# Moving filler matmuls, two input loads and a row of weight loads in a fused spectral-mixer and MLP training step

## The chip, the cores and the metric

The kernel runs on one core of a Trainium2 chip. The metric is the device time of one execution in microseconds (us), taken as the median of several runs. Before the change three runs gave 359.58, 359.83 and 359.80 us, a median of 359.8 us.

## The reference

The reference computes one block of a network and all its gradients. `S` is 2048 and `D` is 448, everything is in bf16.

```
def _A_ref(x, w_r, w_i):                      # spectral mixer
    X = rfft2(x); X = X * (w_r + 1j * w_i); return irfft2(X)
def _B_ref(x, w1, b1, w2, b2):                # MLP over the token axis
    h = layernorm(x)
    u = gelu(einsum("bsd,sf->bdf", h, w1) + b1)
    return transpose(einsum("bdf,fs->bds", u, w2) + b2)
h  = x + _A_ref(layernorm(x), A_w_r, A_w_i)
h2 = h + _B_ref(layernorm(h), B_w1, B_b1, B_w2, B_b2)
# outputs: h2 and the gradients of x, w_r, w_i, w1, b1, w2, b2 for a given grad_out
```

## The kernel before

**Tiling.** A Fourier transform of length 2048 over the tokens is done in two steps with small matrices. The first step works on 16 "rows" `t` (128 tokens each): `row_a(t)` multiplies the folded row with a 128x128 matrix, `row_b(h)` multiplies the result with the cosine and sine tables `csF`. The results are copied out of PSUM and sent by a DMA from one layout in SBUF to another, into `D2` (line 668, eight DMAs; the fifth to eighth read from `rX`). The second step is `s2_stage` (line 671). It works on four sets `s`; for each set, `four` issues 48 small matmuls of 32x32 on `D2` into four PSUM tiles, these are copied out as `x`, VectorE multiplies them with the spectral weights into `y` (`w_mult`, eight operations for each set), and a second `four` does the inverse step of the set on `y`. The result is copied out and sent by DMA into `D3` (line 697, four DMAs for each set). `inv_rows` then reads `D3`, and every row of it needs all four sets.

The backward pass runs the same stages once more on the gradient, with `bwd_mult` in place of `fwd_mult`: eight further VectorE operations for each set give the gradient of the spectral weights.

**Order of the work.** TensorE, VectorE, ScalarE and the DMA queue of SyncE (SP) run in the order in which the program is written. Nearly all DMAs stand in SP's one queue, the transposing loads too, and an instruction that waits there holds all that is behind it. Which of VectorE and ScalarE copies a PSUM tile out is decided by a planner (`Meter`, `evac`), from estimated loads. Reshuffle DMAs are put into SP's queue a little later than their data is asked for (`defer`, 1.1 us of the program's own clock, which advances with each matmul that is written).

**Fillers.** `fill(n)` issues the next `n` steps of work that is independent of the stage at hand. In the forward pass that is `dg_gen` (line 791): 14 blocks of 16 matmuls of 128x448, 224 steps in all. Block `j` reads the transposed weight tile `w2T` number `j`, and when it is finished its buffer is loaded with a later tile (five buffers; past the eighth load, the loads are held back until line 907 and are then put into the queue). After the four sets, `fill(24)` and `drain()` issue whatever is left. In the backward pass the fillers are `gw_gen` (line 1228): 15 units of 28 steps with matmuls of up to 512 columns, 420 steps, whose results are copied out and stored to DRAM. `drain()` after the last inverse row issues what is left of these.

**Numbers that place the fillers.** `s2_stage(get_x, on_mult, n1, n2, gap)` issues, for each `s` from 0 to 4: the `four` of set `s`, `fill(n1)`, the inverse `four` of set `s-1`, the weight product of set `s`, `fill(n2)`; and `fill(gap)` at the end. So `n1` fillers stand ahead of each inverse `four`, and `n2` behind it.

Before the change the forward steps are used so: 87 up to and with the `fill(6)` of line 905, 5 x (8 + 10) = 90 in the sets, and 47 in `fill(24)` and `drain()`. In the backward pass: 24 in the last rows, 30 before the sets, 5 x (14 + 22) + 24 = 204 in the sets and after them, 16 x 8 = 128 in `inv_rows`, and 34 in the last `drain()`.

**Loads at the start.** `load_x(q)` (line 313) loads a quarter of x (four rows, 448 KB) and `load_w2T` (line 306) loads and transposes a 512 KB tile. VectorE takes the statistics of rows 6 and 7 at step `t = 0` of the row loop, those of rows 8 and 9, the first of `load_x(2)`, at `t = 1` (`STATS`, line 858). `W_AT` (line 860) says how many of the 18 loads of the spectral weights (line 573) are put into the queue at each step of the row loop.

## Time and profile before

| | us |
|---|---|
| median of three runs | 359.8 |
| time of the profiled execution | 358.56 |
| its span, first to last instruction | 356.8 |
| TensorE matmul busy (x2810) | 331.0 (93%) |
| VectorE busy | 251.1 (70%) |
| ScalarE busy | 196.6 (55%) |
| DMA moved | 78.03 MB, mean 219 GB/s |
| mean granted TensorE clock | 0.981 |

Times within the profile are counted from the first instruction, so they end at 356.8; the execution's own time is 1.76 us longer than the span. In the profile's lines PE is TensorE, DVE is VectorE, ACT is ScalarE, SPq is SyncE's DMA queue. Tiles stand under the names of their SBUF regions: `r<-rX` is a reshuffle into `D2`, `r<-r` at line 697 one into `D3`; `ps_mm<-rC,rE` and `ps_mm<-rC,rO` are the forward fillers, which read `w2T` from `rE` or `rO`; `rX` is also the region of `x`, and `rS` that of `y`. Helpers record their callers' work under one line: 218 for ordinary matmuls, 223 for the 32x32 ones of `four`, 82 for ScalarE and VectorE.

### The profile page before, as it was taken

To read this page: it belongs to the slowest core of one execution; us is meant where nothing else is said; L and a number is where in the kernel's file an instruction comes from. 1 tells how busy PE (TensorE), PEld (TensorE's weight loads), DVE (VectorE), ACT (ScalarE), POOL (GpSimd) and SP (SyncE) were. 2 spreads that over 40 slices of the span, in tenths; PEclk is the share of its full clock that TensorE was granted. 3 is DMA by queue.
4 is the path that set the end of the run, shared out by engine and by line. 5 is a ranking of instruction groups with operands and counts; after the bars stand their busy time and mean duration, and the time that the engine had idled before them with its cause. 6 is when DMAs were issued, how large, how long until landed. Compare 5 with 4: busy or idle time off the path is not lost.

```text
span 356.8 us, 7788 instructions
## 1 busy us (share of the span) xinstructions
PE 331.0 (93%) x2810; PEld 173.6 (49%) x2819; DVE 251.1 (70%) x666; ACT 196.6 (55%) x431; POOL 63.6 (18%) x219
## 2 busy tenths in 40 slices
PE   8569929989999999999999999999999999999992
PEld 3336615445654555555555555564334344466541
DVE  8897426871594788858323888877497986489993
ACT  5448533543796653532331245557468786488972
POOL 5767000000122000001000211110000000046761
PEclk9989978999999999999999999999999999999998
DMA  8998898856995999779785789774988998999864
GB/s 206 287 198 193 165 252 183 173 109 197 317 260 218 296 347 253 173 193 287 170 206 148 169 186 181 169 128 144 248 233 211 267 262 253 238 296 271 268 241 155
DMA packets 147247, 78.03 MB, mean 219 GB/s; under 512 B 95688, under 2 KB 139976, under 8 KB 147080
## 3 DMA queue, kind: packets, MB, share of 16 engines
q1 hardware_dynamic: 146920, 77.13, 84.6%
q8 instruction: 22, 0.36, 0.4%
q10 hardware_dynamic: 288, 0.39, 0.3%
q14 instruction: 17, 0.14, 0.1%
HBM read 25.71 MB, written 22.04 MB: 134 GB/s over the span
## 4 chain that ended last, share of the span: by engine, by line
PE 77%; DVE 7%; SPq 5%; ACT 4%; issue 2%; DMA 2%; DVEq 0%; POOL 0%; ACTq 0%
PE ps_mm L218 65%; PE ps_ff L218 8%; DVE r L82 4%; PE ps_ff L223 3%; SPq L306 3%; ACT rO L82 2%; DVE rS L82 2%; DMA rA<-in_A_x_dram 1%; SPq L573 1%; DVE rA L82 1%; DMA r<-rX 1%; ACT rX L82 1%; SPq L316 1%; SPq L668 1%; ACT rAT L82 0%
## 5 line engine op out<-in xcount | busy, mean ns | idle before, releaser
L218 PEld LDWEIGHTS <-r 128*128 128x128 bf16 (+2 forms) x600 | 56.0, 105 | 44.9 <-issue 2.3
L218 PEld LDWEIGHTS <-rS 128*128 128x128 bf16 (+2 forms) x496 | 40.2, 98 | 39.7 <-issue 6.3
L218 PE MATMUL ps_mm<-rD,r 128*128 128x448 bf16 x224 | 44.5, 352 | 0.0
L82 ACT CAST rO<-ps_mm 128x512 bf16<-128x512 f32 (+1 forms) x66 | 35.5, 583 | 14.4 <-PE ps_mm L218 11.8
L218 PEld LDWEIGHTS <-rst 128*128 128x128 bf16 (+1 forms) x320 | 23.5, 97 | 30.7 <-issue 13.6
L218 PE MATMUL ps_mm<-rC,rE 128*128 128x448 bf16 x144 | 33.4, 369 | 2.0 <-DMA rC<-in_grad_out_dram 1.9
L218 PE MATMUL ps_mm<-rB,r 128*128 128x448 bf16 x160 | 31.2, 352 | 0.1
L218 PE MATMUL ps_mm<-rG,rst 128*128 128x512 bf16 (+1 forms) x122 | 26.7, 380 | 0.5 <-issue 0.3
L82 ACT CAST r<-ps_ff 128x452 bf16<-128x452 f32 x41 | 22.6, 587 | 8.2 <-PE ps_ff L223 5.9
L218 PE MATMUL ps_mm<-r,rst 128*128 128x512 bf16 (+2 forms) x144 | 27.1, 345 | 0.0
L82 DVE SCALAR_TENSOR_TENSOR r<-ps_mm,b2col,r 128x448 bf16<-128x448 f32 x16 | 10.9, 682 | 19.9 <-PE ps_mm L218 16.9
L82 ACT ACTIVATE r<-ps_mm,rstd_h 128x448 bf16<-128x448 f32 x16 | 10.2, 634 | 26.8 <-PE ps_mm L218 26.8
L82 ACT ACTIVATE r<-rC 128x448 bf16<-128x448 bf16 x16 | 9.1, 571 | 26.7 <-DMA out_dram<-r 21.1
L82 ACT ACTIVATE rG<-rG 128x896 bf16<-128x896 bf16 x14 | 13.3, 950 | 14.9 <-DVE rG L82 14.7
L218 PE MATMUL ps_mm<-rE,rS 128*128 128x448 bf16 x112 | 21.5, 352 | 0.0
L218 PEld LDWEIGHTS <-rO 128*128 128x128 bf16 (+1 forms) x165 | 15.2, 98 | 12.3 <-ACT rO L82 0.2
L82 ACT CAST rS<-ps_ff 128x512 bf16<-128x512 f32 x31 | 17.9, 581 | 5.3 <-PE ps_ff L218 5.0
L218 PEld LDWEIGHTS <-rE 128*128 128x128 bf16 x144 | 13.9, 102 | 13.1 <-issue 4.3
L82 ACT CAST rG<-ps_mm 128x512 bf16<-128x512 f32 (+1 forms) x33 | 16.5, 544 | 6.6 <-PE ps_mm L218 6.4
L1135 POOL TENSOR_SCALAR lcol<-lcol 128x1 f32<-128x1 f32 x16 | 8.5, 529 | 64.7 <-ACT r L82 64.7
L218 PE MATMUL ps_ff<-csI,rAT 113*128 113x224 bf16 (+1 forms) x108 | 19.0, 298 | 0.6 <-ACT rAT L82 0.4
L1308 POOL TENSOR_SCALAR lcol<-lcol 128x1 f32<-128x1 f32 x16 | 5.3, 332 | 75.9 <-ACT r L82 75.8
(189 smaller groups left out, 606.0 us busy)
## 6 DMA issues: line engine op xcount, KB each, us to landing
out_dram<-rO SPq DMA_DIRECT2D x34, 256.0 KB
r<-in_B_w_dram SPq DMA_DIRECT2D x5, 1024.0 KB
r<-r SPq DMA_DIRECT2D x32, 113.0 KB
rS<-in_B_w_dram SPq DMA_DIRECT2D x4, 896.0 KB
r<-r SPq DMA_DIRECT2D x12, 226.0 KB
out_dram<-rG SPq DMA_DIRECT2D x10, 256.0 KB
rO<-in_B_w_dram SPq DMA_DIRECT2D x2, 1024.0 KB
rC<-in_grad_out_dram SPq DMA_DIRECT2D x4, 448.0 KB
```

The source lines that it names most:

```text
L82: fn(**kw)
L218: nc.tensor.matmul(out, lhsT=lhsT, rhs=rhs, start=start, stop=stop)
L223: nc.tensor.matmul(out, lhsT=lhsT, rhs=rhs, start=start, stop=stop)
L306: nc.sync.dma_start_transpose(out=wT, in_=B_w2[j * P:(j + 1) * P, :].rearrange("f (t c) -> f t c", c=P))
L316: nc.sync.dma_start(out=go_tp[:, 4 * q:4 * q + 4, :], in_=go_tp_d[:, 4 * q:4 * q + 4, :])
L573: nc.sync.dma_start(out=d_ap if store else sb, in_=sb if store else d_ap)
L668: defer(RESH_LAG, lambda: resh[0].dma_start(out=D2[u:u + 125:4, 8 * e:8 * e + 8].rearrange("p g c k -> p (g c k)"), in_=cs.rearrange("p x ...
L1135: gp_.tensor_scalar(out=m1, in0=ms, scalar1=-1.0 / D, scalar2=None, op0=ALU.mult)
L1308: gp_.tensor_scalar(out=m1, in0=ms, scalar1=-2.0 / D, scalar2=None, op0=ALU.mult)
```

## The change

1. The third and fourth quarters of x are asked for ahead of the second and third `w2T` tiles; before, each came behind one of them.
2. The loads of the spectral weights start at step 0 of the row loop in place of step 1, so that each stands one step earlier; there are 18 as before.
3. Thirty fillers are issued between the rows and the first forward set, and `n1` of the forward sets is 9 in place of 8. The sum of steps is fixed: 117 now stand before the sets, 5 x (9 + 10) = 95 in them, and 12 are left for `fill(24)` and `drain()`, 35 fewer than before.
4. In the backward sets `n1` is 13 in place of 14 and `n2` is 20 in place of 22. That is 15 steps fewer in the sets; the last `drain()` has 49 in place of 34.

```diff
     load_go(2)
     load_go(3)
+    load_x(2)
+    load_x(3)
     load_w2T()
-    load_x(2)
     load_w2T()
-    load_x(3)
     gtail = rst[0:16, 2 * P:3 * P]
...
-    W_AT = {t: 2 if t % 2 else 1 for t in range(1, 13)}
+    W_AT = {t: 1 if t % 2 else 2 for t in range(12)}
...
     while held_w2:
         held_w2.pop(0)()
+    fill(30)
...
-    s2_stage(lambda s: set_of(Xs, s), fwd_mult, 8, 10, 0)
+    s2_stage(lambda s: set_of(Xs, s), fwd_mult, 9, 10, 0)
     sc.activation(out=warm, in_=eps_h, func=ACT.Sqrt)
     fill(24)
     drain()
...
-    s2_stage(lambda s: X_ring.next(), bwd_mult, 14, 22, N_FILL_B[4], ...
+    s2_stage(lambda s: X_ring.next(), bwd_mult, 13, 20, N_FILL_B[4], ...
```

More of the change, by code (lines that the diff above doesn't have):

```diff
@@ L1287 @@
     Meter.slack = 7.0
-    s2_stage(lambda s: X_ring.next(), bwd_mult, 14, 22, N_FILL_B[4], {0: lambda: load_du(1), 1: lambda: (load_du(0), load_xall(0)), 2: lambda: load_xall(1), 3: lambda: load_du(2)},
+    s2_stage(lambda s: X_ring.next(), bwd_mult, 13, 20, N_FILL_B[4], {0: lambda: load_du(1), 1: lambda: (load_du(0), load_xall(0)), 2: lambda: load_xall(1), 3: lambda: load_du(2)},
              2.0 * INV_SD)
```

## The prediction

> **What bounds the kernel now.** I read the page's busy slices first (8.92 us each), then TensorE's waits, then SP's queue and TensorE's timeline around the longest wait, last the sums over stretches.

> ```profile
> PE   8569929989999999999999999999999999999992
> PEclk9989978999999999999999999999999999999998
> ```

> TensorE is full from slice 7 on. It is idle in the first three slices and above all in slice 6 (44.6 to 53.5 us). The granted clock is low there and just behind. TensorE's waits name the cause:

> ```profile
> PE ps_ff L223 <- DMA r<-rX: 6.9, 1, 6.9
> PE ps_ff L218 <- DVE rX L82: 3.0, 1, 3.0
> ```

> The first is the start of the forward sets, which wait for `D2`; the second is row 5 of the row loop. SP's queue shows why `D2` is late (start, length, line):

> ```profile
> 44.96 1.91 SPq L573 DMA_DIRECT2D rW<-in_A_w_i_dram  x3
> 46.97 0.58 SPq L668 DMA_DIRECT2D r<-r  x1
> 47.60 1.91 SPq L573 DMA_DIRECT2D rW<-in_A_w_i_dram  x3
> 49.61 2.57 SPq L668 DMA_DIRECT2D r<-rX  x4
> 52.28 4.24 SPq L306 DMA_TRANSPOSE rO<-in_B_w_dram  x2
> 57.56 5.71 SPq L306 DMA_TRANSPOSE rE<-in_B_w_dram  x2
> 63.37 2.89 SPq L697 DMA_DIRECT2D r<-r  x4
> ```

> SP issues without a gap from 0.73 us on, so the reshuffles that TensorE finished computing at 44.5 go out at 49.6 to 52.2. At the other end of the sets:

> ```profile
> 78.86 0.38 PE L223 MATMUL ps_ff<-rS,UVT 32*32 32x452 bf16 x16 [1.14 <-DVE rS L82]
> 79.50 7.93 PE L218 MATMUL ps_mm<-rC,rE 128*128 128x448 bf16 x41
> 87.27 3.19 PE L218 MATMUL ps_mm<-rC,rO 128*128 128x448 bf16 x16
> 90.29 0.83 PE L218 MATMUL ps_ff<-RTm,r 128*113 128x128 bf16 x12
> ```

> The last inverse group ends at 79.5, then 57 fillers (10 of `n2`, 47 left over) run for 10.8 us, 0.19 us each, and only then `inv_rows` starts, though the last `D3` reshuffle had landed at 88.4 (the trace's DMA semaphores). So fillers are short at 46.6 and in surplus at 79.5. From 107 on TensorE is busy in nearly every microsecond, so a start of `inv_rows` that is earlier moves everything behind it. The stretches below (PE busy first) show the clock, then the backward pass:

> ```profile
> 19.18:22.59 3.41, 1.01 (x10) 0.74 (x11) 3.19 (x12) 0.89 (x1) 2.60 (x11) 1.00 0.82 199
> 22.59:26.00 3.41, 3.40 (x16) 1.71 (x14) 3.34 (x14) 2.12 (x4) 1.35 (x8) 0.50 1.02 197
> 53.31:56.72 3.41, 3.23 (x54) 1.78 (x55) 2.14 (x4) 0.97 (x2) 0.00 (x0) 0.50 0.99 225
> 278.70:288.70 10.00, 9.79 (x148) 4.03 (x149) 8.88 (x19) 7.79 (x16) 0.00 (x0) 1.00 0.90 265
> 307.50:341.30 33.80, 33.80 (x259) 19.62 (x258) 29.95 (x90) 27.62 (x72) 18.02 (x51) 1.00 0.99 278
> ```

> A stretch in which TensorE was busy 30% (19.18 to 22.59) is followed by one at half clock; the stretch before it, busy 1.91 of 3.42 us, 56%, was not. The half clock at 53.31 costs the first set some 1.5 us.

> **x ahead of w2T.** In the trace DMAs land in the order of issue: the last `load_go` 13.99, w2T 1 at 16.8, x 2 at 18.2, w2T 2 at 20.2, x 3 at 22.0. A quarter of x takes 1.2 to 1.4 us when it follows a plain load, a w2T 2.1 to 2.9. After the change: x 2 at 15.3, x 3 at 16.5, w2T 1 at 19.1, w2T 2 at 21.3. VectorE, idle from 16.83 to 18.24 for x 2, goes on 1.4 us earlier. But TensorE meets its second filler block at 17.07, and that needs w2T 1: it now waits 2.0 us, and `row_b(0)`, two fillers and `row_a(5)` are queued behind. `row_a(5)` was at 21.58 and has its operand at 20.1. The half-clock stretch should move from 22.59 to 19.18. Together TensorE is 0 to 1.4 us ahead in the rows. None of it is on the path, because SP sets when `D2` lands. [...]

> **Weight loads a step earlier.** 18 issues of 0.61 us. They precede the fifth `D2` reshuffle in both orders, so SP has the same work ahead of the seventh, which set 0 needs (issued 50.98, landed 53.36). Nothing gained; the sets start at 53.5. Bounds: 0.7 us earlier (w2T 2 lands at 21.3 where x 3 landed at 22.0) and 0.4 later (the small loads go out at 19.2, not 18.85).

> **Thirty fillers before the sets.** 30 x 0.19 = 5.7 us, from 46.6 or up to 1.4 earlier, so to 50.9 to 52.3. They read w2T 5 to 7, loaded by 47. Of the 6.9 us wait 1.2 to 2.6 us stay. The filler time itself is taken from the surplus behind the sets, so its worth is counted there. The clock: 49.9 to 53.3 would then be busy 30 to 70%, between the row that dropped (30%) and the one that didn't (56%), mostly nearer to the second; I take full clock, and 1.5 us for the other end. [...]

> The fillers also call for w2T 10 to 13 sooner: SP now has six transposing loads in a row at 52.3, where two stood between `D3` reshuffles. Four of them took 1.87 to 2.18 us each: 52.3 + 6 x 2.0 = 64.3 for the reshuffles of set 0 (63.4 before), + 2.9, + 3.4 for the bias transposes, + 2.9, + 2.9 = 76.4 behind set 2. Set 3 asks at 78, so SP is free by then; before it was not (its reshuffles of sets 2 and 3 went out in one run from 79.19 to 84.75).

> **The sets.** VectorE sets their pace: from one `y` to the next are the rest of an inverse group, 0.68 us, two copies 1.16, products 3.9, together 5.67 (67.47, 73.14, 78.81). TensorE's 18 fillers and two groups are about 5.1, so a ninth filler at `n1` goes into its waits (0.39, 0.32, 1.14). Only in set 0 does TensorE set the pace: at full clock 53.5 + 0.7 + 19 x 0.19 + 0.7 + 9 x 0.19 = 60.2 for the first inverse group, in place of 61.5; y of set 3 then at 77.3, last group ended at 78.0. At half clock it is 79.75.

> **The drain.** 22 fillers, 4.2 us, end at 82.2. `D3` of set 3: first copy done 78.6, four issues of 0.71 to 81.45, landing 2.7 to 3.6 us after the last (88.39 - 84.75 with the w1 loads right behind, as they will be): 84.2 to 85.1. I take 85.1, the row in the same place. So TensorE waits some 2.9 us for `D3` and `inv_rows` starts at 85.15 in place of 90.29: **-5.1 us** (-5.9 with the early landing; -3.4 at half clock). If that wait empties a clock stretch, `inv_rows` pays up to 1.5 us.

> **Backward sets.** TensorE is busy 9.79 of 10.0 us in a set; VectorE's own loop (6.93 from copies to `y`, 1.93 for the rest of the weight gradient) is 8.9. Three fillers of 0.216 us fewer make TensorE's set 9.35, still the longer. So the sets end 15 x 0.216 = 3.2 us earlier, and `drain()` after the last row is 3.2 us longer: TensorE's sum is unchanged, and it was the last to end (350.5, with VectorE's row chain at 350.65, which now ends sooner). At the junction the last `D3` landed at 306.7 for a start at 307.5; two fillers (0.4 us) fewer cover it, and SP is issuing without a gap there. I take **+0.3 us**, bounds -0.3 (end of VectorE's chain) and +1.0. The planner may hand copies to the other engine; one misplaced in VectorE's forward loop is 0.6 us, taken at nothing.

> **Sum.** 358.56 - 5.1 + 0.3 = 353.8 for a profiled execution; the median of the runs stood 1.24 above it: **355.0 us**.

> **Rivals.** (a) Both waits that remain cost clock: the first set stays at half clock (-3.4) and `inv_rows` starts with 1.5 us lost: 359.8 - 3.4 + 1.5 + 0.3 = 358.2. For it: the row at 30%; against it: both waits are shorter than that one. (b) The backward sets turn out to wait for VectorE: they do not shorten, and the 3.2 us come on top of the end: 358.2. Against it: 0.45 us of slack for each set by the sum above, 1.4 us at the last one (y at 296.31, group at 297.67). (c) Slower: SP. Six transposing loads, 16 reshuffles of 0.71, biases 3.4 and landing 3.6 make `inv_rows` start at 52.3 + 6T + 18.5; this passes 90.29 at T = 3.25 us. At T = 3.7, the longest in the row stage, it starts at 93.0: 362.5 us. For it: 3.37, 3.51, 3.68 and even 6.88 were seen beside other traffic; against it: 2.0 for the four in this very place.

> **How the numbers follow.** Forecast 0.66, (a) 0.16, (b) 0.09, (c) 0.09. Low end: early landing, `D2` 0.7 sooner: 359.8 - 6.6 + 0.3 = 353.5. The high end takes in (a) and (b) at 358.2; (c) stays outside. Differences below 0.2% (0.7 us) can't be told from none; (a) and (b) reach into that in part, so 0.84 faster, 0.07 same, 0.09 slower.

> **What would show it.** Right: the 6.9 us wait down to 1 to 3; a new wait of about 2 us for `rE` near 17; full clock at 53 to 57; VectorE's 5.67 us loop unchanged; a new wait of 1 to 3 us of `ps_ff` at line 218 for a DMA `r<-r` near 82; the backward drain longer and the sets shorter by about 3 us each. Wrong: the sets starting later than 54, transposing loads of over 3 us each after 52, or backward sets still 10.0 us long.

## The result, and the profile after

The changed kernel takes 355.59 us (median of 353.49, 355.19, 355.99 and 356.05); the kernel before took 359.69 us beside it. The ratio is 0.9884, 95% interval 0.9836 to 0.9931. A second measurement of both, with more runs, gave 0.989 (0.9855 to 0.9924). So 4.1 us are gone where 4.8 were forecast, and the forecast of 355.0 us is 0.6 us off. The split behind it is not what was forecast: about half of the gain comes from a place to which the forecast gave 0.3 us at most.

The profiled execution took 355.19 us with a span of 353.4 (before 358.56 and 356.8). First the busy slices of the page after, 8.84 us each:

```profile
PE   8579989984999999999999999999999999999995
PEclk9989999998799999999999999999999999999999
```

The hole in slice 6 (2 tenths before) is filled. A new one stands in slice 10 (79.5 to 88.4 us, 4 tenths), and the low clock has moved to it and to the slice behind it. The last slice is at 5 tenths instead of 2: the span ends sooner after TensorE's last matmul. TensorE's waits after:

```profile
PE ps_ff L218 <- DMA r<-r: 5.0, 1, 5.0
PE ps_mm L218 <- DMA rE<-in_B_w_dram: 2.3, 1, 2.3
...
PE ps_ff L223 <- DMA r<-rX: 1.4, 1, 1.4
```

The wait for `D2` fell from 6.9 to 1.4 us, the 3.0 us wait of row 5 is gone, and 2.3 us for the second `w2T` tile are new. The longest one now is `inv_rows` waiting 5.0 us for `D3`. TensorE's timeline around the forward sets:

```profile
45.81 5.84 PE L218 MATMUL ps_mm<-rC,rE 128*128 128x448 bf16 x30
53.04 0.62 PE L223 MATMUL ps_ff<-r,Vt 32*32 32x452 bf16 x16 [1.38 <-DMA r<-rX]
...
78.30 1.31 PE L218 MATMUL ps_mm<-rC,rE 128*128 128x448 bf16 x6
79.44 3.19 PE L218 MATMUL ps_mm<-rC,rO 128*128 128x448 bf16 x16
87.59 1.50 PE L218 MATMUL ps_ff<-RTm,r 128*113 128x128 bf16 x12 [4.96 <-DMA r<-r]
```

The thirty fillers lie in the hole, 22 are left behind the last inverse group, and `inv_rows` starts at 87.59, where it started at 90.29. SP's queue over the same time:

```profile
51.91 4.25 SPq L306 DMA_TRANSPOSE rO<-in_B_w_dram  x2
56.26 9.14 SPq L306 DMA_TRANSPOSE rE<-in_B_w_dram  x3
...
73.45 9.01 SPq L697 DMA_DIRECT2D r<-r  x12
82.56 4.07 SPq L926 DMA_DIRECT2D r<-in_B_w_dram  x2
```

The last twelve `D3` reshuffles leave in one run that ends at 82.47, and right behind them go the first loads of W1, 1 MB each. The chain that ended last shows what that last reshuffle took from issue to landing, and when the long TensorE stage behind the rows (495 matmuls, called the u stage below) begins:

```profile
81.86 5.39 DMA r<-r
87.25 0.35 issue
87.59 14.96 PE ps_ff L218 x108
...
107.96 94.04 PE ps_mm L218 x495
```

In the chain of the kernel before that stage stands here:

```profile
109.24 94.03 PE ps_mm L218 x495
```

So the forward pass gave 1.3 us in this pair of executions, although `inv_rows` starts 2.7 us earlier. The rest went into the clock, as the stretches after show (PE busy first, granted clock in the third column from the end):

```profile
16.95:20.37 3.42, 1.06 (x8) 0.51 (x8) 3.31 (x12) 0.58 (x1) 2.59 (x12) 1.00 1.25 178
20.37:23.78 3.41, 3.41 (x17) 2.06 (x16) 3.26 (x12) 2.46 (x4) 2.41 (x12) 0.50 0.52 122
51.09:54.50 3.41, 2.03 (x55) 1.21 (x54) 0.63 (x2) 0.71 (x3) 0.00 (x0) 1.00 0.86 264
81.81:85.22 3.41, 0.83 (x5) 0.20 (x3) 0.00 (x0) 0.53 (x1) 0.00 (x0) 1.00 0.62 169
85.22:88.63 3.41, 1.04 (x10) 1.07 (x11) 0.00 (x0) 0.35 (x1) 0.00 (x0) 0.50 1.14 298
88.63:92.05 3.42, 3.42 (x17) 1.91 (x16) 1.24 (x3) 1.64 (x4) 0.23 (x1) 0.50 1.15 288
```

The window with the wait for `D2` is busy 2.03 of 3.41 us and keeps the clock. The two windows with the wait for `D3` are busy 24% and 30%, and the stretch behind each of them runs at half clock. From the start of `inv_rows` to the u stage it takes 20.37 us, where it took 18.95 before: 1.4 us lost.

The backward pass gave the other part, and not in TensorE. From the start of the u stage to the end of TensorE's last matmul it is 241.25 us before and 241.82 after; from there to the end of the span it is 6.3 before and 3.6 after. SP's queue at the end, before:

```profile
345.35 0.81 SPq L1273 DMA_DIRECT2D out_dram<-rO  x2
348.33 2.68 SPq L1335 DMA_DIRECT2D out_dram<-r  x2
351.11 1.13 SPq L1273 DMA_DIRECT2D out_dram<-rG  x2
```

and after:

```profile
343.96 2.67 SPq L1336 DMA_DIRECT2D out_dram<-r  x2
346.75 0.86 SPq L1274 DMA_DIRECT2D out_dram<-rO  x2
348.05 0.82 SPq L1274 DMA_DIRECT2D out_dram<-rG  x2
```

Line 1335 (1336 after) stores the input-gradient rows that VectorE finishes last, lines 1273 and 1274 the last pieces of the fourth output. Before, the last row store could go only at 350.68, once VectorE's row chain had ended at 350.65. Two stores stood behind it until 351.11 and 351.91, VectorE's last copy of a result came only behind the rows as well (350.56 to 351.24), and the last transfer landed at 355.70. After, the row chain ends at 346.28, SP's last store is issued by 348.87, only two stores of ScalarE's queue are later (349.99), and the last transfer lands at 352.43.

### The profile page after: what moved, and what is told of

It is laid out like the page before. It is cut to its first block, busy times and chain, and to the rows that moved or that the text cites. A ratio compares the mean times of both kernels' runs of the same rounds, so it can differ in the third digit from the quotient of the medians.

```text
span 353.4 us, 7799 instructions
## 1 busy us (share of the span) xinstructions
PE 333.7 (94%) x2819; PEld 174.1 (49%) x2819; DVE 251.2 (71%) x667; ACT 196.9 (56%) x430; POOL 63.2 (18%) x219
## 4 chain that ended last, share of the span: by engine, by line
PE 82%; DMA 6%; DVE 4%; SPq 3%; ACT 2%; issue 1%; POOL 0%; DVEq 0%; ACTq 0%
PE ps_mm L218 66%; PE ps_ff L218 13%; DMA rE<-in_B_w_dram 3%; PE ps_ff L223 3%; DVE rS L82 2%; DMA r<-r 2%; DMA rO<-in_B_w_dram 1%; DVE r L82 1%; SPq L306 1%; SPq L573 1%; SPq L316 1%; SPq L668 1%; ACT rX L82 1%; SPq L313 0%; DVE rA L82 0%
## 5 line engine op out<-in xcount | busy, mean ns | idle before, releaser
L218 PEld LDWEIGHTS <-r 128*128 128x128 bf16 (+2 forms) x600 | 56.6, 107 | 50.7 <-issue 9.1
L218 PEld LDWEIGHTS <-rS 128*128 128x128 bf16 (+2 forms) x496 | 40.7, 98 | 36.6 <-issue 7.3
L82 ACT CAST rO<-ps_mm 128x512 bf16<-128x512 f32 (+1 forms) x70 | 37.3, 583 | 15.9 <-PE ps_mm L218 14.5
L218 PE MATMUL ps_mm<-rD,r 128*128 128x448 bf16 x224 | 44.5, 352 | 0.0
L218 PEld LDWEIGHTS <-rst 128*128 128x128 bf16 (+1 forms) x320 | 23.5, 97 | 31.3 <-issue 14.1
L218 PE MATMUL ps_mm<-rC,rE 128*128 128x448 bf16 x144 | 32.5, 360 | 4.1 <-DMA rE<-in_B_w_dram 2.3
L218 PE MATMUL ps_mm<-rB,r 128*128 128x448 bf16 x160 | 31.2, 352 | 0.1
L82 ACT CAST r<-ps_ff 128x452 bf16<-128x452 f32 x41 | 22.7, 587 | 11.5 <-PE ps_ff L223 6.2
L218 PE MATMUL ps_mm<-rG,rst 128*128 128x512 bf16 (+1 forms) x128 | 28.5, 380 | 0.3 <-ACT rO L82 0.3
L218 PE MATMUL ps_mm<-r,rst 128*128 128x512 bf16 (+2 forms) x144 | 27.4, 345 | 0.0
L82 ACT ACTIVATE r<-ps_mm,rstd_h 128x448 bf16<-128x448 f32 x16 | 10.1, 633 | 26.8 <-PE ps_mm L218 26.8
L82 DVE SCALAR_TENSOR_TENSOR r<-ps_mm,b2col,r 128x448 bf16<-128x448 f32 x16 | 10.9, 682 | 19.9 <-PE ps_mm L218 17.0
L82 ACT ACTIVATE r<-rC 128x448 bf16<-128x448 bf16 x16 | 9.1, 572 | 26.7 <-DMA out_dram<-r 20.5
L82 ACT ACTIVATE rG<-rG 128x896 bf16<-128x896 bf16 x14 | 13.3, 950 | 15.0 <-DVE rG L82 14.7
L218 PE MATMUL ps_mm<-rE,rS 128*128 128x448 bf16 x112 | 21.5, 352 | 0.0
L218 PEld LDWEIGHTS <-rO 128*128 128x128 bf16 (+1 forms) x165 | 15.1, 98 | 12.9 <-DMA rO<-in_B_w_dram 0.9
L82 ACT CAST rS<-ps_ff 128x512 bf16<-128x512 f32 x31 | 17.9, 580 | 5.7 <-PE ps_ff L218 5.3
L218 PEld LDWEIGHTS <-rE 128*128 128x128 bf16 x144 | 13.5, 99 | 14.2 <-DMA rE<-in_B_w_dram 2.5
L218 PE MATMUL ps_ff<-csI,rAT 113*128 113x224 bf16 (+1 forms) x108 | 20.3, 313 | 0.0
L1136 POOL TENSOR_SCALAR lcol<-lcol 128x1 f32<-128x1 f32 x16 | 8.5, 529 | 64.7 <-ACT r L82 64.7
L82 ACT CAST rAT<-ps_ff 113x512 bf16<-113x512 f32 x24 | 13.8, 584 | 10.6 <-PE ps_ff L218 10.3
L82 DVE SCALAR_TENSOR_TENSOR rA<-ps_ff,rA 128x448 bf16<-128x448 f32 x16 | 9.9, 619 | 12.0 <-PE ps_ff L218 11.9
```

The costliest lines, as they stand in the source:

```text
L82: fn(**kw)
L218: nc.tensor.matmul(out, lhsT=lhsT, rhs=rhs, start=start, stop=stop)
L1136: gp_.tensor_scalar(out=m1, in0=ms, scalar1=-1.0 / D, scalar2=None, op0=ALU.mult)
```

## The experiments

Each ratio is to the kernel before, run on the same chip in the same session, with its 95% interval.

**One part at a time.** Three kernels, each the kernel before with one part of the change.

```diff
+    fill(30)
...
-    s2_stage(lambda s: set_of(Xs, s), fwd_mult, 8, 10, 0)
+    s2_stage(lambda s: set_of(Xs, s), fwd_mult, 9, 10, 0)
```

> Only the forward fillers are changed: thirty between the rows and the first forward set, nine in place of eight between its sets' parts. Theory from the two traces: the start of inv_rows is set by the last reshuffle of D3, which SP issues behind the six transposes and the bias transposes; it starts near 87.6 us (90.29 before), waits 4 to 5 us for it, loses the full clock for one window (some 1.5 us), and the u stage starts 1.0 to 1.6 us earlier. The end of the kernel still has its late stores, so the time falls by 1.0 to 1.6 us. Rival, the forecast's own split: inv_rows near 85.2 with a wait of 2.9 us, full clock, and 4 to 5 us off the time.

Measured: 0.9931 (0.9911 to 0.9951), 2.5 us off: more than the 1.0 to 1.6 that I read from the two traces, and far less than the forecast's 4 to 5. `inv_rows` starts at 86.96 after a wait of 4.1 us, loses the clock for one window, and the u stage starts at 106.82; the end is as late as before, 6.2 us behind the last matmul. From its timeline and its chain:

```profile
86.96 1.41 PE L218 MATMUL ps_ff<-RTm,r 128*113 128x128 bf16 x12 [4.11 <-DMA r<-r]
```

```profile
106.82 94.03 PE ps_mm L218 x495
```

The single pair of profiles understated the gain: the start of the u stage wanders by up to 2 us between executions of the same forward pass. It is 109.24, 108.95, 110.55 and 110.72 in the four traces with the forward pass of before (the kernel before and three experiments below), mean 109.87, and 107.96, 106.82 and 108.84 in the three with the new forward fillers, mean 107.87: 2.0 us.

```diff
-    s2_stage(lambda s: X_ring.next(), bwd_mult, 14, 22, N_FILL_B[4], ...
+    s2_stage(lambda s: X_ring.next(), bwd_mult, 13, 20, N_FILL_B[4], ...
```

> Only the two counts of the backward sets are changed (13 and 20 in place of 14 and 22). Theory from the two traces: TensorE's last matmul moves by less than 1 us either way, but VectorE's chain of input-gradient rows ends some 3 to 4 us earlier, the last stores of input-gradient rows leave SP's queue before the last stores of the fourth output, and the stretch between the last matmul and the end of the span falls from 6.3 to about 3.7 us: the time falls by 1.5 to 2.5 us. Rival, the forecast's own split: 0.3 us more, between 0.3 less and 1.0 more.

Measured: 0.9942 (0.9922 to 0.9961), 2.1 us off. From the u stage to the last matmul it takes 241.47 us, from there to the end 3.6 us. SP's queue at its end:

```profile
347.18 0.33 SPq L1335 DMA_DIRECT2D out_dram<-r  x1
347.63 0.86 SPq L1273 DMA_DIRECT2D out_dram<-rO  x2
348.92 0.82 SPq L1273 DMA_DIRECT2D out_dram<-rG  x2
```

The last row store is now issued ahead of the last stores of the fourth output, and the forecast's +0.3 falls.

```diff
     load_go(3)
+    load_x(2)
+    load_x(3)
     load_w2T()
-    load_x(2)
     load_w2T()
-    load_x(3)
...
-    W_AT = {t: 2 if t % 2 else 1 for t in range(1, 13)}
+    W_AT = {t: 1 if t % 2 else 2 for t in range(12)}
```

> Only the order of the loads is changed (x ahead of the second transpose of w2, the W loads one position earlier). Theory and forecast agree: a wait of about 2 us for the second transpose near 17 to 20 us, a stretch of half clock that moves forward by some 3 us, the rows about 0.8 us ahead, and then the same wait for D2 before the first forward set, which still starts near 53.5: within 0.5 us of before. Rival: the wait and the clock cost what they seem to, and the time rises by 1 to 2 us.

Measured: 1.0004 (0.9985 to 1.0023). The loads are worth nothing by themselves that this can tell, as forecast. There is no profile of this kernel at its usual time, so where its sets start isn't shown.

**The changed kernel once more.**

> The changed kernel once more, unaltered, to narrow its ratio and to see how far its forward part moves from one execution to the next. If the parts add up (0.9931 for the forward fillers alone, 0.9942 for the backward counts alone, 1.0004 for the loads alone), its ratio is 0.9877, 4.4 us below before; if the load order costs something only in their company, it is above 0.990. The profile should show inv_rows waiting 3.5 to 5 us for the last reshuffle of D3, which lands 4 to 5 us after its issue, and one or two windows of half clock behind it.

Measured: 0.989 (0.9855 to 0.9924). The three parts multiply to 0.9877, so they add up within the interval. Here `inv_rows` waits 3.8 us and starts at 88.98, and the reshuffle that it waits for lands 4.24 us after the end of its issue. The wait for `D2` is 2.2 us in this execution, its window is busy 35%, and the first set lost the clock as it did before the change: a part of why the u stage's start wanders.

**What `inv_rows` waits for.** My first theory was SP's queue: six transposing loads and two bias transposes stand ahead of `D3`'s reshuffles. This is the changed kernel with the bias transposes asked for later:

```diff
     def fwd_mult(s, j, x, y):
-        if (s, j) == (2, 0):
-            turn_biases()
...
     drain()
+    turn_biases()
```

> The changed kernel with the two bias transposes asked for behind the last forward set in place of in the midst of its third set, so that they stand behind the reshuffles of D3 in SP's queue. If SP's queue sets the start of inv_rows: the reshuffles are issued some 2.4 us earlier, inv_rows starts near 85.2 (87.6 in the changed kernel), its wait halves to about 2.5 us, the window may keep the full clock, and the time is 2.4 to 4 us below the changed kernel (351.5 to 353.2 us). If the landing is bound by something else (the DMA engines' own backlog, or the last inverse group at 78.3), inv_rows stays near 87 and the time within 0.5 us of the changed kernel.

Measured: 0.985 (0.9821 to 0.988), 5.4 us off. TensorE's timeline:

```profile
85.05 0.85 PE L218 MATMUL ps_ff<-RTm,r 128*113 128x128 bf16 x12 [2.24 <-issue]
```

The numbers came as expected, but not by the step that I had named. SP did become free early, and then waited from 77.08 to 79.02 for the last set's copies; its last reshuffle went out from 81.67 to 82.28, against 81.86 to 82.47 in the changed kernel, only 0.2 us earlier. It landed at 84.65 instead of 87.25. Two things differ around it. One is what is issued next: the two small transposes of the biases here, W1 there. The other is the pause of 1.9 us in SP's queue ahead of the last four reshuffles, which the changed kernel doesn't have. Stretches of the changed kernel (DMA's busy share and GB/s are the last two columns):

```profile
84.00:86.00 2.00, 0.00 (x0) 0.00 (x0) 0.00 (x0) 0.00 (x0) 0.00 (x0) 0.81 0.97 269
```

and of this one:

```profile
84.00:86.00 2.00, 0.85 (x12) 0.74 (x12) 0.00 (x0) 0.51 (x2) 0.26 (x2) 1.00 0.05 11
```

Two more kernels were made to tell W1 from SP. The first leaves the bias transposes where the changed kernel has them and asks for them a second time, only to hold W1 back:

```diff
     drain()
+    turn_biases()
```

> The changed kernel, its bias transposes left in the third forward set, and the same two transposes asked for a second time behind the last forward set, so that 2.4 us of SP's queue lie between the last reshuffle of D3 and the first load of W1 (1 MB each). Two theories for the run with the bias transposes late, whose last reshuffle of D3 was issued only 0.2 us earlier than in the changed kernel (81.67 to 82.28 against 81.86 to 82.47) but landed 2.6 us earlier (84.65 against 87.25). W1 theory: the loads of W1, issued right behind, share the DMA engines with the reshuffles and delay them; then this run is as good as that one: inv_rows near 85.2, wait near 2.4 us, time near 353.5, 2 us below the changed kernel. SP theory: the place of the bias transposes ahead of the reshuffles counts; then inv_rows stays at 87 to 87.6 and the time at 355.6.

Measured: 353.53 us, ratio 0.9865 (0.9829 to 0.9901). SP's queue, then TensorE:

```profile
74.48 8.46 SPq L697 DMA_DIRECT2D r<-r  x12
83.05 2.35 SPq L786 DMA_TRANSPOSE smc<-rst  x2
85.49 2.60 SPq L927 DMA_DIRECT2D r<-in_B_w_dram  x2
```

```profile
86.03 1.50 PE L218 MATMUL ps_ff<-RTm,r 128*113 128x128 bf16 x12 [2.52 <-DMA smc<-rst]
```

The twelve reshuffles leave in one run as in the changed kernel, and end at 82.95. The last of them lands at 85.69, 2.74 us after the end of its issue, where the changed kernel took 4.78. So with the bias transposes where the changed kernel has them, and without W1 right behind, the last reshuffle lands 2.0 us sooner after its issue. `inv_rows` starts 0.34 us behind that landing, as it did in the changed kernel, and at 86.03 rather than 85.2 because the last set stood 0.7 us later than in the run with the bias transposes late. (The profile puts the wait down to the second bias transposes.)

The second leaves SP as free as in the run with the bias transposes late, and puts W1 right behind the reshuffles again:

```diff
     w1cs = [load_w1c(jp) for jp in range(3)]
+    turn_biases()
```

> The other half of the same question: the bias transposes late, but behind the three loads of W1, so that SP's queue is as free ahead of D3's reshuffles as in the run with the bias transposes late, and the loads of W1 stand right behind the reshuffles as in the changed kernel. W1 theory: the last reshuffle lands near 87, inv_rows starts near 87.3, time near 355.6. SP theory: the landing stays at 84.7, inv_rows at 85.05, time near 353.6.

Measured: 354.51 us, 0.9871 (0.9844 to 0.9899). In the profiled execution `inv_rows` starts at 87.08, as the W1 theory wants, but the last set itself came some 1.8 us late there (its first reshuffle was issued at 80.84, against 79.02), and the last reshuffle landed only 3.04 us after the end of its issue. That is neither theory's number. The landings of the last four reshuffles, by the traces' DMA semaphores, tell more (us from the end of each issue to its landing):

| run | lags of the last four | pause of SP ahead of them | W1 right behind |
|---|---|---|---|
| before | 2.55, 2.47, 2.73, 3.64 | no, a run of 8 | yes |
| changed kernel | 4.35, 3.87, 4.22, 4.78 | no, a run of 12 | yes |
| changed kernel once more | 3.11, 3.18, 3.42, 4.24 | no, 12 | yes |
| forward fillers alone | 3.04, 2.97, 3.03, 4.11 | no, 12 | yes |
| n1 of 5 (below) | 3.21, 3.14, 4.12, 4.98 | no, 12 | yes |
| bias transposes twice | 2.91, 2.83, 2.78, 2.74 | no, 12 | no |
| bias transposes late | 2.47, 1.93, 2.36, 2.37 | yes | no |
| bias transposes late, n1 of 7 (below) | 1.94, 2.38, 2.29, 2.73 | yes | no |
| bias transposes behind W1 | 2.11, 2.21, 2.38, 3.04 | yes | yes |

Both theories had a part. Where W1 stands right behind, the last reshuffle lags 0.6 to 1.1 us more than the one ahead of it; where the small transposes do, the difference is at most 0.4. But in an unbroken run of twelve the lag has grown to some 3 us before W1 is issued, and behind a pause it starts again near 2: that is what SP's early freedom seems to have been worth. The changed kernel's profiled execution has a third part. Its lag rose by 2 us at once, between the landings at 79.48 and 82.19, ahead of W1's first issue at 82.56. From there on one of the eight semaphore updates that tell of a reshuffle's landing came 1.5 to 1.8 us behind the other seven (for the last reshuffle at 87.25, the others by 85.48). What held it back stays open; with one execution of each kernel these shares are rough. The times can't tell the parts from each other: 0.985 and 0.9865 without W1 right behind, 0.9871 to 0.989 with it, and the intervals overlap.

**The clock behind the wait.** The changed kernel with twenty fillers more behind the last inverse group (five calls of four fewer; the expectation counts four of the five calls):

```diff
-    s2_stage(lambda s: set_of(Xs, s), fwd_mult, 9, 10, 0)
+    s2_stage(lambda s: set_of(Xs, s), fwd_mult, 5, 10, 0)
```

> The changed kernel with five in place of nine fillers between the parts of its forward sets: sixteen more (3.0 us) are left to run behind the last inverse group, SP's queue stays as it is. Theory: inv_rows stays near 87.3 (the landing of D3 behind SP's queue), its wait falls from 4.96 to about 1.9 us, the clock stays full, and the u stage starts 18.95 us later, near 106.3 in place of 107.96: 1.1 to 1.7 us below the changed kernel, about 354.2. If the clock cost nothing, the time stays at 355.6; if the fillers were needed in the sets, it rises.

Measured: 354.58 us, 0.9861 (0.9825 to 0.9897), not to be told from the changed kernel. In the profiled execution the reshuffle landed at 88.43, 4.98 us after the end of its issue, so 2.6 us of wait were left and the clock was lost all the same (20.06 us from the start of `inv_rows` to the u stage). It decides nothing on the price. The run that does has the bias transposes late and moves ten fillers (eight in the expectation, by the same miscount):

```diff
-    s2_stage(lambda s: set_of(Xs, s), fwd_mult, 9, 10, 0)
+    s2_stage(lambda s: set_of(Xs, s), fwd_mult, 7, 10, 0)
...
     drain()
+    turn_biases()
```

> The bias transposes stand behind the last forward set, as in the run before, and seven in place of nine fillers stand between the parts of the forward sets, so that eight more (some 1.5 us) are left to run behind the last inverse group. Theory: inv_rows stays at 85.05, set by the landing of D3; its wait falls from 2.24 to about 0.7 us, so the clock is not lost behind it, and the u stage starts 18.95 us after inv_rows (as in the kernel before, at full clock) in place of 20.27: near 104.0, which is 1.3 us less than with nine fillers, time near 352.3 us. Rival: the fillers in the sets hid something, and the last inverse group ends later by what was taken out: no gain, or a loss of up to 1.5 us.

Measured: 351.93 us, ratio 0.9781 (0.9742 to 0.9821), faster than both kernels and the best of the study. Its chain:

```profile
78.39 0.71 PE ps_ff L223 x32
79.10 6.16 PE ps_mm L218 x32
85.36 0.42 PE ps_ff L218 x4
...
104.12 94.03 PE ps_mm L218 x495
```

TensorE goes from the last inverse group through 32 fillers into `inv_rows` without a wait, and from there to the u stage it takes 18.76 us at full clock, against 20.27 with nine fillers in the sets and a 2.2 us wait. The sets lost nothing by the ten fillers. By the traces that is 1.2 us (the u stage at 104.12 instead of 105.32). The ratios, 0.985 and 0.9781, lie 2.5 us apart, more than the traces explain, but their intervals meet.

**Two queues for the last reshuffles.** With the bias transposes late, the last two of the four reshuffles go out from ScalarE's queue:

```diff
+                    eng = nc.scalar if s == 4 and scale is None and i > 1 else resh[0]
-                    defer(RESH_LAG, lambda g=g, ab=ab: resh[0].dma_start(...
+                    defer(RESH_LAG, lambda g=g, ab=ab, eng=eng: eng.dma_start(...
```

> The bias transposes stand behind the last forward set, nine fillers in the sets, and of the four reshuffles of the last forward set the last two go out from ScalarE's queue in place of SP's. Theory: what is left of the wait is SP's issue of four reshuffles (79.02 to 82.28) and the landing 2.4 us after; with two queues the last is issued by 81.5, D3 lands near 83.9, inv_rows starts near 84.2 (85.05 with one queue), its wait falls to 1.4 us, the clock stays full, and the u stage starts near 103.2 in place of 105.3: time near 351.5. Rival: the landing is bound by the transfers themselves, which then share the engines, and inv_rows stays at 85.

Measured: 353.82 us, 0.9822 (0.9794 to 0.985), not to be told from one queue with the same nine fillers (0.985, 0.9821 to 0.988). `D2` came late in the profiled execution (sets at 54.95), and with it all that follows. ScalarE's first issue had to wait for its own copies until 82.95 and took 1.22 us, so its second ended 1.06 us behind SP's second (84.90 against 83.84). Nothing gained by it that can be seen.

**The end of the kernel.** The kernel before, with the last two row stores on GpSimd's queue:

```diff
-                defer(2.0, lambda: nc.sync.dma_start(
+                defer(2.0, lambda: (nc.gpsimd if t >= 13 else nc.sync).dma_start(
```

> The kernel before, with the last two stores of input-gradient rows on GpSimd's queue in place of SP's; nothing else moves. Theory: the end of the kernel before is late because these stores stand in SP's queue, waiting for VectorE's rows, ahead of the last two stores of the fourth output. With them on another queue TensorE's last matmul ends where it did (350.5), the rows end where they did (350.65), and the span ends 1 to 2 us earlier: time 357.3 to 358.3. Rival: the end is set by VectorE itself (its last eviction comes behind the rows) or by the transfers, and the time stays within 0.5 us of before.

Measured: 0.9948 (0.9926 to 0.997), 1.9 us off. SP's queue at its end:

```profile
346.67 0.81 SPq L1273 DMA_DIRECT2D out_dram<-rO  x2
349.33 0.97 SPq L1273 DMA_DIRECT2D out_dram<-rG  x2
```

Nothing stands ahead of the last stores any more. In the profiled execution the stretch behind the last matmul is 5.3 us instead of 6.3; the last row store, now GpSimd's, is issued at 352.75 there, because GpSimd's own small step for the last row came only behind its first store and VectorE had to wait 0.39 us for it. The two edits to the end together:

> The two counts of the backward sets and, with them, the last two stores of input-gradient rows on GpSimd's queue: the two edits that each took 1.9 to 2.1 us off by themselves. If they take away the same wait at the end of the kernel, they don't add up: about 357.2, within 0.6 us of the backward counts alone (ratio 0.993 to 0.996). If each took away something of its own, the ratio is near 0.989, 3.9 us below before.

Measured: 0.9932 (0.9905 to 0.996). They don't add up (0.9942 and 0.9948 alone): both take away the same wait. Behind the last matmul it is 3.8 us, near the 3.6 with the backward counts alone.

## Why the prediction was right or wrong

Its total held (-4.8 forecast, -4.1 measured) because two errors cancelled, and that was luck.

**Right: the front.** The 6.9 us wait fell to 1.4 (forecast 1.2 to 2.6), the sets started at 53.04 (forecast 53.5), and in the profiled execution the first set ran at full clock. That was partly luck too: of the nine traces with the new fillers three lost the clock there, behind windows busy 21%, 30% and 35% (the eleven fillers behind the first group took 3.02, 3.45 and 3.75 us in them, 2.25 in the other six). The wait for the second `w2T` tile is 2.3 us at 17.5 to 19.8 (2.0 forecast), the half-clock stretch moved from 22.59 to 20.37 (forecast 19.18), and the ratio for the loads alone is 1.0004.

**Right: the sets and the drain.** The inverse groups after are 5.67 us apart on average; the last ended at 78.3 (78.0 forecast), the drain at 82.6 (82.2). Some 0.2 us of that is a slip in the forecast's sum: with 60.2 in place of 61.5 the last `y` moves from 78.81 to 77.5, not to 77.3.

**Wrong in size: the start of `inv_rows`**, forecast 85.15, found 87.59. Of the 2.44 us, 1.02 are SP's (the last issue ended at 82.47, not 81.45: the first of four went out 0.57 later, and one took 1.16 us instead of 0.61), 1.14 are the landing (4.78 us behind the issue, not 3.64, the one row that I had; most of the difference was there before W1 was issued, for the reshuffle ahead of the last lags 4.22 where it lagged 2.73), and about 0.3 the time from landing to the first matmul. The six transposing loads took 2.6 us each on average where I had 2.0, the DMA engines being full from 56 to 68 (busy share 1.08 there), but that delay was all but used up by the time set 3 asked: its first reshuffle went out at 79.17, and at 79.02 where SP was free. Rival (c) therefore never came near.

**Wrong in place: the clock.** I wrote that `inv_rows` may pay up to 1.5 us if the wait emptied a clock stretch, and kept it out of the sum. It paid 0.9 to 1.4 us in the three traces with the new fillers (19.86 to 20.37 us to the u stage against 18.95). A wait of 2.9 us can empty most of a window of 3.4, as the 3.0 us wait in the trace of before did (19.18 to 22.59, busy 30%), so the loss had to stand in the sum with a chance. This is the half of rival (a) that came true here. The windows don't lie the same in these executions: their edges near `inv_rows` are at 85.22, 87.07 and 85.68 in the three with the new forward fillers, and one or two windows are lost. In the trace after they were lost behind windows busy 24% and 30%.

So the forward part is 2.0 us (means of the traces) to 2.5 us (times), not 5.1.

**Wrong: the end of VectorE's chain.** TensorE's own part of the backward pass was right: from the u stage to the last matmul it takes 241.25 to 241.27 us in the three traces with the old counts and 241.47 to 241.97 in nine of the ten with the new ones (242.55 in the tenth), 0.2 to 0.7 us more, where +0.3 was forecast. The sets are shorter by 0.4 to 0.6 us each and the drain is 3.1 us longer. TensorE stays full in both, as the stretches after show (PE busy first: 9.75 of 10 us in the sets, all of 33.8 in the rows):

```profile
275.00:285.00 10.00, 9.75 (x136) 3.73 (x136) 9.06 (x21) 8.32 (x17) 0.00 (x0) 1.00 0.83 246
304.09:337.89 33.80, 33.80 (x264) 19.99 (x265) 30.20 (x92) 27.99 (x73) 18.52 (x53) 1.00 0.97 261
```

But I priced VectorE's earlier end at 0.3 us at most, the most that I thought the end of its chain could give. Its end also held its own last copy and SP's queue with the last stores: 6.3 us behind the last matmul became 3.6. That is 2.5 to 2.7 us that the forecast lacked. The 6.3 us stood in the trace of before, where the span ended at 356.8 and TensorE at 350.5, and I didn't ask what filled them.

## What to carry to other kernels

Follow the last microseconds behind the busiest engine as carefully as the stretch that the change is about: a store that waits for the last result holds every store behind it in the same queue (here one that could go only at 350.68 held two until 351.11 and 351.91). When fillers are moved from a surplus into a hole, leave as many as cover the transfer that the next stage waits for, for a short wait can also cost the clock of the stage behind it (here one of 2.24 us cost 1.3, one of 4.96 us 1.4); the kernel that left ten more, and issued two small transposes behind that transfer instead of ahead of it, was 1% faster than the change. And when an experiment gives the number that a theory foretold, check in its trace that the step which the theory names really moved, and look at the landings of the transfers ahead of it as well.

## What the runs showed of the hardware

The last 113 KB reshuffle of a run lagged 0.6 to 1.1 us more than the one ahead of it, from the end of its issue to its landing, in the six traces of the table above in which 1 MB loads were issued right behind it on the same queue, and at most 0.4 us more in the three in which two small transposes were. In the unbroken runs of twelve the reshuffles ahead of the last lagged 2.8 us and more, behind a pause of the queue 1.9 to 2.5.

Six transposing loads of 512 KB in a row took 15.6 us, 2.6 each, in the changed kernel (51.91 to 67.49), with a DMA busy share of 1.05.
